# Moving the shifted copies of score bits from GpSimd to VectorE in a two-attention kernel

## The chip, the cores and the metric

The kernel runs on one core of a Trainium2 chip. The time is the device time of one execution in microseconds (us). Before the change three runs gave 713.89, 715.19 and 715.36 us; their median is 715.19 us. The profile is of one further execution, whose span is 713.4 us.

## The reference

Two attention layers with 2048 positions, model width 448 and 16 heads of 28 are computed and laid side by side in the output.

```python
# A: 16 query heads share one key head and one value head
q = heads(x @ wq); k = x @ wk; v = x @ wv
p = softmax(q @ k.T * 28 ** -0.5)           # over all 2048 keys
a = (p @ v).reshape(1, 2048, 448) @ wo
# B: each position looks at itself and 7 earlier ones, 2 apart
q, k, v = heads(x @ wqkv)
logits = where(idx >= 0, q . k[idx] * 28 ** -0.5, -1e9)   # idx = pos - 2 * (0..7)
b = (softmax(logits) @ v[idx]).reshape(1, 2048, 448) @ wo
out = concatenate([a, b], axis=-1)
```

Inputs and output are bf16.

## The kernel before

Attention A is done in 16 *groups*: four chunks of 512 queries by four sets of four heads. A group has 64 *jobs*, one per head and block of 128 keys. A job is one score matmul (line 1119) that fills one PSUM bank with 128 keys by 512 queries; the four heads sit in four strips of 32 rows, so that up to four jobs run side by side in the array. A 29th row of the operands adds a term from the query's squared norm (line 652 squares it); the key side holds a one in that row.

A bank of scores goes one of two ways. ScalarE takes the exponential of three banks or of two banks in one activation (line 924) into the tile P. VectorE instead builds the exponential from bits: line 1155 adds a bias to the scores, clips at zero and stores int16 values, which read as bf16 are powers of two with a straight line between them. Three *shifted copies* of these bits, plus 32, plus 64 and plus 96, are made in tile Z: line 1163 makes the first from the base (512 elements in each partition), and line 1170 makes the other two from the first two (1024 elements). Each of the four versions goes through a value matmul with its own weighted set of values, and the four sums together approximate the exponential closely. So a job on ScalarE costs TensorE one value matmul (line 1218) and a job on VectorE four. Banks 0 to 2 and 3 to 4 are two rings for ScalarE; banks 5 to 7 are *flexible* and serve VectorE's score banks, the value sums and the projections. The tile P has 8 slots and Z has 6. About every fourth or fifth bank goes to VectorE (DRATE, line 34, and `want_d`, line 1132).

Attention B has 16 such groups as well, with banded masks added by a matmul (line 1078) and small score matmuls (line 1092). Its key eviction (line 688) multiplies by a column that blanks the unused rows and adds a column that puts the one into each head's 29th row; the columns are operands in SBUF. Query evictions (line 658) multiply by such a column too.

At the end of a group the value sums are copied out (line 728), the denominators go by small transfers through a reciprocal (line 747) and back as a broadcast, a product normalizes them (line 778), four output projections follow, and their results are cast (line 818) and stored.

No loop of the chip sets the order. A planner in Python keeps a clock for each engine and lets the engine with the earliest clock choose its next piece of work (`loop`, line 856). Work is listed with the engines that may do it, a priority and a planned duration in nanoseconds. Each engine then runs its list strictly in the planned order, and waits on semaphores where an operand comes from another engine. Planned durations that are off therefore do not make a result wrong, but leave an order that does not fit. For the first copy the plan says 560 on GpSimd and 215 on VectorE, and for the second 1.7 times that; squares have 620 and normalizations 1150 on GpSimd (GP_S1, GP_TT16, GP_TT32, lines 42 to 44). GpSimd or VectorE may take these, VectorE only when GpSimd's clock is far ahead (`hold`, in `spec_choose`, line 876). TensorE chooses in `pe_choose` (line 1270): a score batch whose banks are free goes first, and the rest fills the time until ScalarE would run dry.

Of the kernel before, what the change touches and what calls it, by code (L numbers as in the profile page):

```python
# [15 lines left out]
DH = 28  # L16
# [21 lines left out]
TOL = 40.0  # L38
FTOL = 250.0
EXPC = 0.8333  # L40
EXP0 = 52.0
GP_S1 = 560.0
GP_TT16 = 620.0
GP_TT32 = 1150.0
# [40 lines left out]
class Spec:  # L85


    def __init__(self, engs, reads, writes, make, prio, dur, gate, name, hold):
        self.engs = engs
        self.reads = reads  # L90
        self.writes = writes
        self.make = make
        self.prio = prio
        self.dur = dur
        self.gate = gate
        self.name = name
        self.hold = hold

# [32 lines left out]
class _Gen:  # L131
    def __init__(self, nc, A_x, A_wq, A_wk, A_wv, A_wo, B_x, B_wqkv, B_wo, out):
        self.nc = nc
        self.A_x, self.A_wq, self.A_wk, self.A_wv, self.A_wo = A_x, A_wq, A_wk, A_wv, A_wo
        self.B_x, self.B_wqkv, self.B_wo = B_x, B_wqkv, B_wo
        self.out = out
        self.ops = []
        self.T = {e: 0.0 for e in ("pe", "act", "dve", "gp", "sp")}
        self.mode = None
        self.pend = []  # L140
        self.fills = []
        self.cur = None
        self.actq = []
# [16 lines left out]
    def put(self, eng, emit, dur, took, reads=(), writes=(), appends=(), dma=False, name=""):  # L160
        o = Op()
        o.eng, o.emit, o.dma, o.name = eng, emit, dma, name
        deps = {}
        for res in reads:
            for d in res.w:
                deps[d] = True
        for res in writes:
            for d in res.w:
                deps[d] = True
            for d in res.r:  # L170
                deps.setdefault(d, False)
        for res in appends:
            for d in res.r:
                deps.setdefault(d, False)
        t = self.T[eng]
        for d, full in deps.items():
            if d.eng != eng or d.dma:
                t = max(t, d.done + SEM)
            elif full and eng != "pe":
                t = max(t, d.done + SELF)  # L180
        o.deps = [d for d, full in deps.items() if d.eng != eng or d.dma or (full and eng != "pe")]
        o.start = t
        o.done = t + took
        self.T[eng] = t + dur
        o.busy = dur

        def note(lst):
            if not dma:
                for i, x in enumerate(lst):
                    if x.eng == eng and not x.dma:  # L190
                        lst[i] = o
                        return
            lst.append(o)

        for res in reads:
            note(res.r)
        for res in writes:
            res.w = [o]
            res.r = []
        for res in appends:  # L200
            note(res.w)
        o.idx = len(self.ops)
        self.ops.append(o)
        return o
# [109 lines left out]
    def alloc(self, es):  # L314
# [47 lines left out]
        self.zero = sb([128, 512], BF16, "zero")  # L362

# [5 lines left out]
    def plan_start(self):  # L369
        g = self  # L370
        put = self.put
        self.nswitch = 0
        R = {}
# [69 lines left out]
        for c in range(1, 4):  # L443
            for kt in range(4):
                c0 = 128 * kt if kt < 3 else D - 128
                self.dma_op("sp", g.xT_A[:, kt, 512 * c:512 * c + 512], g.A_x[0, 512 * c:512 * c + 512, c0:c0 + 128],
                            writes=[res("xA", c, kt)], transpose=True, issue=760, lands=2800, name="xAt")
        for c in range(4):
            par, half = c // 2, c % 2
            for kt in range(4):  # L450
                c0 = 128 * kt if kt < 3 else D - 128
                src = g.B_x[0, 1024 * half + par:1024 * half + 1024 - 1 + par:2, c0:c0 + 128]
                self.dma_op("sp", g.xT_B[:, kt, 512 * c:512 * c + 512], src,
                            writes=[res("xB", c, kt)], transpose=True, issue=760, lands=2800, name="xBt")

        def later():
# [7 lines left out]
            w3("gp", g.wB, g.B_wqkv, 0, 3 * D, "wB", [])  # L464
            gp(lambda e: e.memset(g.mask[:, :], 0.0), 450, writes=[res("m")])
# [28 lines left out]
    def evict(self, bank, make, engs=("dve",), dur=(600,), reads=(), writes=(), prio=2, last=True, cb=None, name=""):  # L494

        rd, wr = [bank.res] + list(reads), list(writes)

        def mk(eng, ns):
            if last:
                bank.busy = False  # L500
            return dict(emit=make, reads=rd, writes=wr, took=ns + 95, cb=cb)
        self.pend.append(Spec(engs, rd, wr, mk, prio, dict(zip(engs, dur)), None, name, False))

    def later(self, engs, dur, reads, make, prio=3, gate=None, name="", hold=False, writes=()):
        self.pend.append(Spec(engs, list(reads), list(writes), make, prio, dict(zip(engs, dur)), gate, name, hold))
# [10 lines left out]
    def make_fills(self):  # L516
# [30 lines left out]
        for c in range(4):  # L547
# [5 lines left out]
            def after(bank, c=c):  # L553
                self.evict(bank, lambda e: e.tensor_scalar(out=g.kT_A[:, 512 * c:512 * c + 512], in0=g.bank(bank.i), scalar1=g.col[:, 0:1],
                                                           scalar2=None, op0=ALU.add), ("dve",), (600,), reads=[res("c0")], writes=[res("kA", c)],
                           prio=0.5 if c == 0 else 1, name="ke")
# [71 lines left out]
        def q_fill(kind, key, s, gg, w, off, x, xk, c, due, enabled, elig=0.0):  # L628
# [10 lines left out]
            def after(bank):  # L639
                def cb(o):  # L640
# [13 lines left out]
                    if first and gg == 0:  # L654
                        self.later(("dve",), (345,), [res(r1, s, gg)], mk, prio=0.4, name="sq")
                    else:
                        self.later(("gp", "dve"), (GP_TT16, 345), [res(r1, s, gg)], mk, prio=2.5, name="sq", hold=True)
                self.evict(bank, lambda e: e.tensor_scalar(out=t[:, s, gg, :], in0=g.bank(bank.i), scalar1=g.col[:, 2:3], scalar2=None, op0=ALU.mult),  # L658
                           ("dve",), (600,), reads=[res("c2")], writes=[res(r1, s, gg), res(r2, s, gg)], prio=0.5 if first and gg == 0 else 2,
# [15 lines left out]
        for c in range(4):  # L675
# [3 lines left out]
            for gg in range(4):  # L679
# [7 lines left out]
                def after(bank, gg=gg, c=c):  # L687
                    self.evict(bank, lambda e: e.tensor_scalar(out=g.kT_B[:, gg, 512 * c:512 * c + 512], in0=g.bank(bank.i), scalar1=g.col[:, 1:2],  # L688
                                                               scalar2=g.col[:, 0:1], op0=ALU.mult, op1=ALU.add), ("dve",), (600,),
                               reads=[res("c0"), res("c1")], writes=[res("kB", c, gg)], prio=2, name="kBe",  # L690
                               cb=lambda o: self.kready.add((c, gg)))
                fill(f"kB{c}.{gg}", t0 - 13 + 4 * gg, steps, after, elig=t0 - 50)
            q_norms("B", c % 2, ("B", c), t0 - 6)
            for b in range(5):
# [11 lines left out]
                def after(bank, nk=nk, vs=vs, c=c, b=b):  # L706
                    self.evict(bank, lambda e: e.tensor_copy(out=g.vB[0:nk, vs, :, 0:DH],  # L707
                                                             in_=g.bank(bank.i, 0, nk, 0, D).rearrange("p (h d) -> p h d", d=DH)),
                               ("dve",), (540,), reads=[res("vB1")], writes=[res("vB", vs)], prio=2, name="vBe",
# [9 lines left out]
    def chain(self, key, bank, due):  # L719
# [44 lines left out]
        def mul(p, b):  # L764
            ok = (kind, c)

            def mk(eng, ns):
# [4 lines left out]
                def cb(o):  # L772
# [3 lines left out]
                    if self.odone[ok] == 4:  # L776
# [4 lines left out]
                       hold=True)  # L781
# [94 lines left out]
    def spec_choose(self, eng):  # L876
        T = self.T[eng]
        best = None
        for s in self.pend:
# [4 lines left out]
            if eng == "dve" and s.hold and T > self.T["gp"] - GP_AHEAD:  # L884
                continue
            if self.ready(eng, s.reads, s.writes) <= T + 15.0:
                best = s
# [6 lines left out]
    def do_spec(self, s, eng):  # L894
# [9 lines left out]
        else:  # L904
            op = self.put(eng, a["emit"], ns, a["took"], a["reads"], a["writes"], name=s.name)
# [111 lines left out]
    def qk_next(self):  # L1017
        ring = self.rings[self.ringi % 2]
        bj = self.b_next() if len(ring) == 2 else None
        if bj is not None:  # L1020
            jobs, kind = bj, "B"
            s = bj[0] % 2
            reads = [self.res("qB", s, bj[1]), self.res("qrB", s, bj[1]), self.res("kB", bj[0], bj[1]), self.res("m"), self.res("m0"), self.res("id")]
            if bj[0] % 2:
                reads.append(self.res("kB", bj[0] - 1, bj[1]))
# [38 lines left out]
    def do_qk(self, jobs, kind, reads):  # L1064
# [37 lines left out]
        dj = None  # L1102
        if self.want_d(T):
            ok = self.flex_free(T + 10)
            if ok:
                dj = self.d_job({j for _, _, j in jobs}, jobs)
        alljobs = list(jobs)
# [29 lines left out]
    def dread(self, job, bank):  # L1137
# [11 lines left out]
        def mk(eng, ns):  # L1149
            bank.busy = False  # L1150

            def cb(o):
                unit(0, zr[0])
                self.later(("gp", "dve"), (GP_S1, 215), [zr[0]], sh1, prio=1.2, name="s1", hold=True, writes=[zr[1]])
# [4 lines left out]
        def sh1(eng, ns):  # L1159
            def cb(o):  # L1160
                unit(1, zr[1])
                self.later((eng,), (ns * 1.7,), [zr[0], zr[1]], sh2, prio=1.1, name="s2", writes=[zr[2]])
            return dict(emit=lambda e: e.tensor_scalar(out=g.Z[:, z, 1, :], in0=g.Z[:, z, 0, :], scalar1=32.0, scalar2=None, op0=ALU.add),  # L1163
                        reads=[zr[0]], writes=[zr[1]], took=ns + 60, cb=cb)

        def sh2(eng, ns):
# [3 lines left out]
            return dict(emit=lambda e: e.tensor_scalar(out=g.Z[:, z, 2:4, :], in0=g.Z[:, z, 0:2, :], scalar1=64.0, scalar2=None, op0=ALU.add),  # L1170
# [99 lines left out]
    def pe_choose(self):  # L1270
        T = self.T["pe"]
        q = self.qk_next()
        if q is not None and q[1] and q[0] <= T + 30.0:
            self.do_qk(q[2], q[3], q[4])
            return
        idle = self.T["act"] + sum(EXPC * 512 * len(b) + EXP0 for b, _, _ in self.actq)
# [6 lines left out]
        room = horizon - T - sw  # L1283
        if pv and (len(pv) == 4 or press) and (room >= 217.0 - TOL or hard):
# [57 lines left out]
```

## Time and profile before

| engine | busy us | share | instructions |
|---|---|---|---|
| TensorE matmuls | 503.2 | 71% | 5268 |
| VectorE | 290.6 | 41% | 496 |
| ScalarE | 433.5 | 61% | 369 |
| GpSimd | 642.5 | 90% | 369 |

| operation | on | count | mean ns |
|---|---|---|---|
| first copy, line 1163 | GpSimd | 134 | 1503 |
| first copy, line 1163 | VectorE | 42 | 623 |
| second and third copy, line 1170 | GpSimd | 134 | 2783 |
| second and third copy, line 1170 | VectorE | 42 | 675 |
| score bits, line 1155 | VectorE | 176 | 688 |
| exponential, line 924 | ScalarE | 365 | 1247 |

The second table comes from the profile's groups: each has a line, an engine, an operation, the tiles written and read, and the mean duration of one instruction. Matmuls on TensorE are pipelined, so that their busy time holds latencies that overlap. The mean granted clock of TensorE was 0.756 of its full speed. An idle engine is not by itself a loss; what counts is what the engines that others wait for are waiting for.

### The profile page before, as it was taken

What the parts mean: (1) busy time and instruction counts of PE and PEld (TensorE: products, weight loads), DVE (VectorE), ACT (ScalarE), POOL (GpSimd) and SP (SyncE); (2) the same over time, 40 slices, a digit from 0 to 9 for tenths busy, and PEclk for the clock granted to TensorE, in tenths of its full rate; (3) what the DMA queues carried; (4) which work ended last, traced back from release to release, by engine and by line L of the source; (5) the groups of instructions that cost most, each with busy time, mean ns of one, the idle gap of its engine ahead of it and who ended that gap; (6) DMA issues with size and microseconds to landing.
All of it is one profiled execution on the core that took longest, in us unless ns stands there. A gap on an engine that the chain in (4) does not pass through costs nothing.

```text
span 713.4 us, 12414 instructions
## 1 busy us (share of the span) xinstructions
PE 503.2 (71%) x5268; PEld 141.2 (20%) x5268; DVE 290.6 (41%) x496; ACT 433.5 (61%) x369; POOL 642.5 (90%) x369
## 2 busy tenths in 40 slices
PE   6967775876788677779757658684758856556672
PEld 3311221211222122123212212221112201111111
DVE  5634514442542335325344625224433415364431
ACT  2965766664876567559758739374657636455450
POOL 7799949999699999998799999998999999999960
PEclk9988978886987678569989969677576865555556
DMA  9920001010010101001010100011001010000001
GB/s 180 142 53 17 2 1 41 10 33 1 18 54 28 35 1 33 2 17 36 24 32 28 34 16 17 7 30 38 10 24 36 8 42 0 10 7 1 16 1 42
DMA packets 37335, 20.10 MB, mean 28 GB/s; under 512 B 27552, under 2 KB 32736, under 8 KB 37280
## 3 DMA queue, kind: packets, MB, share of 16 engines
q1 hardware_dynamic: 35616, 16.84, 9.9%
q0 software_dynamic: 704, 2.03, 1.5%
q8 instruction: 42, 0.69, 0.4%
q10 hardware_dynamic: 960, 0.43, 0.3%
q14 instruction: 13, 0.11, 0.1%
HBM read 11.31 MB, written 3.93 MB: 21 GB/s over the span
## 4 chain that ended last, share of the span: by engine, by line
POOL 80%; PE 11%; issue 4%; DVE 3%; DMA 1%; POOLq 0%; ACTq 0%; ACT 0%; SPq 0%
POOL Z L1170 48%; POOL Z L1163 26%; PE ps L512 4%; POOL oTn L778 3%; PE ps L1218 3%; POOL sq L652 3%; PE ps L1119 2%; DVE Z L1155 1%; DMA bc<-rec_scratch 1%; DMA wq<-in_A_wq_dram 1%; PE ps L1078 1%; DVE qT_A L658 0%; PE ps L1092 0%; DVE PVs L728 0%; DVE ob L818 0%
## 5 line engine op out<-in xcount | busy, mean ns | idle before, releaser
L924 ACT ACTIVATE P<-ps 128x1536 bf16<-128x1536 f32 x365 | 431.0, 1247 | 253.4 <-PE ps L1119 204.4
L1170 POOL TENSOR_SCALAR Z<-Z 128x1024 int16<-128x1024 int16 x134 | 372.9, 2783 | 9.3
L1218 PE MATMUL ps<-Z,vA 128*32 128x512 bf16 x704 | 193.9, 493 | 126.7 <-POOL Z L1163 80.4
L1163 POOL TENSOR_SCALAR Z<-Z 128x512 int16<-128x512 int16 x134 | 201.4, 1503 | 21.3 <-DVE Z L1155 21.3
L1218 PE MATMUL ps<-P,vA 128*32 128x512 bf16 x848 | 191.6, 471 | 30.7 <-POOL Z L1170 18.1
L1155 DVE TENSOR_SCALAR Z<-ps 128x512 int16<-128x512 f32 x176 | 121.0, 688 | 223.4 <-PE ps L1119 223.0
L1119 PE MATMUL ps<-qT_A,kT_A 29*128 29x512 bf16 x1024 | 157.1, 465 | 12.1 <-DVE Z L1155 3.9
L1218 PEld LDWEIGHTS ps<-Z,vA 128*32 128x32 bf16 x704 | 40.2, 101 | 190.3 <-POOL Z L1163 87.1
L1119 PEld LDWEIGHTS ps<-qT_A,kT_A 29*128 29x128 bf16 x1024 | 34.4, 94 | 165.3 <-issue 80.2
L1218 PEld LDWEIGHTS ps<-P,vA 128*32 128x32 bf16 x848 | 40.7, 98 | 86.1 <-issue 40.7
L512 PE MATMUL ps<-xT_B,wB 128*32 128x512 bf16 x512 | 51.2, 447 | 1.0 <-DVE kT_B L688 0.8
L778 POOL TENSOR_TENSOR oTn<-PVs,bc 128x512 bf16<-128x512 f32 x24 | 30.5, 1272 | 14.1 <-DMA bc<-rec_scratch 14.1
L728 DVE COPY PVs<-ps 128x512 f32<-128x512 f32 x32 | 21.8, 687 | 49.9 <-PE ps L1218 35.5
L512 PE MATMUL ps<-woA,oTn 128*32 128x448 bf16 x256 | 26.8, 473 | 17.6 <-POOL oTn L778 17.4
L818 DVE CAST ob<-ps 128x448 bf16<-128x448 f32 x32 | 19.9, 621 | 44.8 <-PE ps L512 44.8
L1170 DVE TENSOR_SCALAR Z<-Z 128x1024 int16<-128x1024 int16 x42 | 28.3, 675 | 0.9
L512 PE MATMUL ps<-wB,xT_B 128*32 128x448 bf16 (+3 forms) x320 | 27.6, 413 | 0.2 <-DVE PVs L728 0.2
L1163 DVE TENSOR_SCALAR Z<-Z 128x512 int16<-128x512 int16 x42 | 26.2, 623 | 1.1
L512 PE MATMUL ps<-woB,oTn 128*32 128x448 bf16 x256 | 21.9, 406 | 5.3 <-POOL oTn L778 4.6
L1078 PE MATMUL ps<-mask,ident 128*128 128x512 bf16 x64 | 25.0, 482 | 0.1
L512 PE MATMUL ps<-xT_A,wq 128*32 128x512 bf16 x256 | 23.3, 428 | 0.6 <-DMA wq<-in_A_wq_dram 0.4
L707 DVE CAST vB<-ps 109x448 bf16<-109x448 f32 (+2 forms) x20 | 12.4, 618 | 24.6 <-PE ps L512 24.6
(81 smaller groups left out, 241.9 us busy)
## 6 DMA issues: line engine op xcount, KB each, us to landing
bc<-rec_scratch SPq DMA_DIRECT2D x32, 256.0 KB
out_dram<-ob SPq DMA_DIRECT2D x32, 112.0 KB, 1.7
den<-PVs SPq DMA_DIRECT2D x128, 2.0 KB, 1.7
wB<-in_B_wqkv_dram POOLq DMA_DIRECT2D x1, 1008.0 KB, 7.2
rec_scratch<-rec SPq DMA_DIRECT2D x32, 8.0 KB, 1.6
xn<-in_A_x_dram SPq DMA_DIRECT2D x4, 112.0 KB, 2.2
woA<-in_A_wo_dram POOLq DMA_DIRECT2D x4, 98.0 KB, 4.0
woB<-in_B_wo_dram POOLq DMA_DIRECT2D x4, 98.0 KB, 5.5
```

What stands on the lines that cost most here:

```text
L512: ins = e.matmul(self.bank(bank, 32 * j, 32 * j + m, 0, n), lhs(j), rhs(j), start=start, stop=stop, tile_position=(0, 32 * j))
L652: return dict(emit=lambda e: e.tensor_tensor(out=g.sq[:, z, gg, :], in0=t[:, s, gg, :], in1=t[:, s, gg, :], op=ALU.mult), reads=[res(r1, s ...
L728: return dict(emit=lambda e: e.tensor_copy(out=g.PVs[:, p, :], in_=g.bank(bank.i)), reads=[bank.res], writes=[self.pvs.res[p]], took=ns + ...
L778: return dict(emit=lambda e: e.tensor_tensor(out=g.oTn[:, z, gg, :], in0=g.PVs[:, p, :], in1=g.bc[:, b, :], op=ALU.mult), reads=[self.pvs. ...
L818: return dict(emit=lambda e: e.tensor_copy(out=g.ob[:, o_, :], in_=g.bank(bank.i, 0, 128, 0, D)), reads=[bank.res], writes=[self.outs.res[ ...
L924: self.put("act", lambda e: e.activation(g.P[:, k, 0:512 * n], g.ps[:, lo:lo + 512 * n], ACT.Exp, scale=ASCALE), ns, ns + 110, [self.banks ...
L1078: ins = e.matmul(g.bank(b), g.ident[:, :], (g.mask if half else g.mask0)[:, :], start=True, stop=False)
L1119: ins = e.matmul(g.bank(b), g.kT_A[32 * j:32 * j + DH + 1, 128 * tb:128 * tb + 128], g.qT_A[32 * j:32 * j + DH + 1, gr.sc % 2, gr.g, :], s ...
L1155: return dict(emit=lambda e: e.tensor_scalar(out=g.Z[:, z, 0, :], in0=g.bank(bank.i), scalar1=ZBIAS, scalar2=0.0, op0=ALU.add, op1=ALU.max ...
L1163: return dict(emit=lambda e: e.tensor_scalar(out=g.Z[:, z, 1, :], in0=g.Z[:, z, 0, :], scalar1=32.0, scalar2=None, op0=ALU.add), reads=[zr ...
L1170: return dict(emit=lambda e: e.tensor_scalar(out=g.Z[:, z, 2:4, :], in0=g.Z[:, z, 0:2, :], scalar1=64.0, scalar2=None, op0=ALU.add), reads ...
L1218: ins = e.matmul(g.bank(b, 32 * j, 32 * j + 32), l, r, start=st, stop=sp, tile_position=(0, 32 * j))
```

## The change

The shifted copies are made by VectorE, except for those of every twelfth bank (GP_EACH), which GpSimd makes. The planner is told that the two engines exclude each other in the copies, the squares and the normalizations (`port`: such an operation starts only after the last one of either engine), and is given other durations for GpSimd. The copies are written as a multiplication by one and an addition in one instruction. Query evictions use an immediate factor in place of a column (except in the first chunk), and B's key eviction becomes a plain copy, after which a small transfer writes the ones into the 29th rows. In `pe_choose` a score batch whose banks are free may wait for a flexible bank, so that a job for VectorE can go along with it, as long as ScalarE's backlog lasts (DWAIT); and a projection that was begun is carried on first if there is time. In the changed program 175 pairs of copies are on VectorE and 16 on GpSimd, and ScalarE has 359 exponentials.

```diff
+DWAIT = 100.0
-GP_S1 = 560.0
-GP_TT16 = 620.0
-GP_TT32 = 1150.0
+GP_S1 = 900.0
+GP_EACH = 12
+GP_TT16 = 1010.0
+GP_TT32 = 1230.0
...
     def put(self, eng, emit, dur, took, reads=(), writes=(), appends=(), dma=False, name="", port=False):
+        if port:
+            t = max(t, self.port)
+            self.port = t + dur
...
-                        self.later(("gp", "dve"), (GP_TT16, 345), [res(r1, s, gg)], mk, prio=2.5, name="sq", hold=True)
-                self.evict(bank, lambda e: e.tensor_scalar(out=t[:, s, gg, :], in0=g.bank(bank.i), scalar1=g.col[:, 2:3], scalar2=None, op0=ALU.mult),
+                        self.later(("gp", "dve"), (GP_TT16, 345), [res(r1, s, gg)], mk, prio=2.5, name="sq", hold=True, port=True)
+                sc1 = g.col[:, 2:3] if first else CQ
+                self.evict(bank, lambda e: e.tensor_scalar(out=t[:, s, gg, :], in0=g.bank(bank.i), scalar1=sc1, scalar2=None, op0=ALU.mult),
...
-                    self.evict(bank, lambda e: e.tensor_scalar(out=g.kT_B[:, gg, 512 * c:512 * c + 512], in0=g.bank(bank.i), scalar1=g.col[:, 1:2],
-                                                               scalar2=g.col[:, 0:1], op0=ALU.mult, op1=ALU.add), ("dve",), (600,),
+                            return dict(dma=True, out=g.kT_B[DH:128:32, gg, 512 * c:512 * c + 512], in_=g.one[0:4, :], reads=[res("one"), res("kB", c, gg)],
+                                        writes=[res("k1B", c, gg)], cb=lambda o: self.kready.add((c, gg)))
+                    self.evict(bank, lambda e: e.tensor_copy(out=g.kT_B[:, gg, 512 * c:512 * c + 512], in_=g.bank(bank.i)), ("dve",), (600,),
...
+            if s.port and eng in ("dve", "gp") and self.port > T + 15.0:
+                continue
...
-                self.later(("gp", "dve"), (GP_S1, 215), [zr[0]], sh1, prio=1.2, name="s1", hold=True, writes=[zr[1]])
+                en = ("gp",) if self.nD % GP_EACH == 5 else ("dve",)
+                self.later(en, (GP_S1 if en[0] == "gp" else 200,), [zr[0]], sh1, prio=1.2, name="s1", writes=[zr[1]], port=True)
...
-                self.later((eng,), (ns * 1.7,), [zr[0], zr[1]], sh2, prio=1.1, name="s2", writes=[zr[2]])
-            return dict(emit=lambda e: e.tensor_scalar(out=g.Z[:, z, 1, :], in0=g.Z[:, z, 0, :], scalar1=32.0, scalar2=None, op0=ALU.add),
+                self.later((eng,), (332 if eng == "dve" else 1.9 * ns,), [zr[0], zr[1]], sh2, prio=1.1, name="s2", writes=[zr[2]], port=True)
+            return dict(emit=lambda e: e.tensor_scalar(out=g.Z[:, z, 1, :], in0=g.Z[:, z, 0, :], scalar1=1.0, scalar2=32.0, op0=ALU.mult, op1=ALU.add),
...
-            return dict(emit=lambda e: e.tensor_scalar(out=g.Z[:, z, 2:4, :], in0=g.Z[:, z, 0:2, :], scalar1=64.0, scalar2=None, op0=ALU.add),
+            return dict(emit=lambda e: e.tensor_scalar(out=g.Z[:, z, 2:4, :], in0=g.Z[:, z, 0:2, :], scalar1=1.0, scalar2=64.0, op0=ALU.mult, op1=ALU.add),
...
+        idle = self.T["act"] + sum(EXPC * 512 * len(b) + EXP0 for b, _, _ in self.actq)
         if q is not None and q[1] and q[0] <= T + 30.0:
-            self.do_qk(q[2], q[3], q[4])
-            return
-        idle = self.T["act"] + sum(EXPC * 512 * len(b) + EXP0 for b, _, _ in self.actq)
+            if (q[3] == "B" or T + 40.0 > idle - QKLAT - DWAIT or not self.want_d(T) or self.flex_free(T + 10)
+                    or self.d_job({j for _, _, j in q[2]}, q[2]) is None):
+                self.do_qk(q[2], q[3], q[4])
+                return
+            q = (idle - QKLAT - DWAIT,) + q[1:]
...
+        if self.cur is not None and f is not None and room >= self.cur.list[self.cur.i][2] - TOL and not hard:
+            self.do_fill(f)
+            return
```

## The prediction

> **What bounds the kernel now.** I read five views in this order. First the page's busy times, slices and chain.
>
> ```profile
> PE 503.2 (71%) x5268; PEld 141.2 (20%) x5268; DVE 290.6 (41%) x496; ACT 433.5 (61%) x369; POOL 642.5 (90%) x369
> ...
> POOL 7799949999699999998799999998999999999960
> PEclk9988978886987678569989969677576865555556
> ...
> POOL 80%; PE 11%; issue 4%; DVE 3%; DMA 1%; POOLq 0%; ACTq 0%; ACT 0%; SPq 0%
> POOL Z L1170 48%; POOL Z L1163 26%; PE ps L512 4%; POOL oTn L778 3%; PE ps L1218 3%; POOL sq L652 3%; PE ps L1119 2%; DVE Z L1155 1%; DMA bc<-rec_scratch 1%; DMA wq<-in_A_wq_dram 1%; PE ps L1078 1%; DVE qT_A L658 0%; PE ps L1092 0%; DVE PVs L728 0%; DVE ob L818 0%
> ```
>
> GpSimd works 90% of the span, full in nearly every slice, and 80% of the chain that ended last is GpSimd; three quarters of the span is two lines, 1170 and 1163, the shifted copies. Second, the cost groups for those lines on both engines:
>
> ```profile
> L924 ACT ACTIVATE P<-ps 128x1536 bf16<-128x1536 f32 x365 | 431.0, 1247 | 253.4 <-PE ps L1119 204.4
> L1170 POOL TENSOR_SCALAR Z<-Z 128x1024 int16<-128x1024 int16 x134 | 372.9, 2783 | 9.3
> ...
> L1163 POOL TENSOR_SCALAR Z<-Z 128x512 int16<-128x512 int16 x134 | 201.4, 1503 | 21.3 <-DVE Z L1155 21.3
> ```
>
> One pair of copies costs GpSimd 1.50 + 2.78 = 4.28 us, and 134 pairs cost 574 us. Its idle time ahead of them is 31 us, so it is simply full. Third, the waits:
>
> ```profile
> ACT P L924 <- PE ps L1119: 204.4, 109, 8.6
> PEld ps L1218 <- POOL Z L1163: 103.0, 37, 7.8
> ...
> PEld ps L1218 <- POOL Z L1170: 80.2, 50, 3.2
> ```
>
> TensorE's queue is in order: a value matmul (line 1218) that waits for a Z copy holds back the score matmuls (1119) behind it, so ScalarE starves for 204 us. GpSimd's backlog becomes idle time of TensorE and ScalarE. Fourth, what VectorE pays for the same two operations, per line the shortest, median and longest in ns:
>
> ```profile
> L1163 DVE TENSOR_SCALAR Z<-Z x42: 277/542/1179, 14.1 to 683.1; 128x512 int16<-128x512 int16 x42
> L1170 DVE TENSOR_SCALAR Z<-Z x42: 378/668/1369, 14.4 to 683.8; 128x1024 int16<-128x1024 int16 x42
> ```
>
> Even its slowest copy beats GpSimd's. In the trace many first copies took 0.29 us and many second ones 0.43 us; the longer ones met a GpSimd operation. Fifth, slices of 20 us (busy us and instruction counts in the order PE, weight loads, DVE, ACT, POOL, then clock): all seven whose granted clock is above 0.9, that is where TensorE was least starved.
>
> ```profile
> 20.00:40.00 20.00, 16.78 (x311) 5.91 (x303) 14.14 (x31) 18.88 (x17) 14.92 (x14) 0.97 0.93 135
> 100.00:120.00 20.00, 16.53 (x216) 5.27 (x204) 10.22 (x18) 16.74 (x15) 15.82 (x9) 0.92 0.07 16
> 200.00:220.00 20.00, 16.00 (x202) 4.88 (x199) 7.93 (x13) 15.21 (x14) 19.61 (x11) 0.93 0.14 44
> 260.00:280.00 20.00, 17.26 (x220) 5.44 (x220) 10.69 (x18) 17.88 (x17) 18.06 (x10) 0.99 0.07 19
> 320.00:340.00 20.00, 18.55 (x253) 6.18 (x251) 11.18 (x19) 18.96 (x18) 16.94 (x9) 0.96 0.13 39
> 340.00:360.00 20.00, 16.46 (x200) 5.10 (x200) 7.87 (x14) 15.84 (x15) 15.60 (x10) 0.91 0.06 16
> 380.00:400.00 20.00, 15.90 (x225) 5.13 (x224) 11.84 (x21) 16.76 (x16) 19.48 (x10) 1.00 0.12 35
> ```
>
> ScalarE does 17+15+14+17+18+15+16 = 112 exponentials there, 16.0 per 20 us, and up to 18; over the whole span it does 365 x 20 / 713 = 10.2. That is the gap to close.
>
> **What the Trainium skill says.** "VectorE: DVE Perf Modes", The perf-mode tier table: a tensor_scalar on 16-bit data in SBUF can run at 4 elements a cycle. The trace agrees in kind: 512 more elements add 0.13 to 0.15 us (0.28 or 0.29 against 0.41 to 0.43), a quarter of what one element a cycle at that page's 0.96 GHz would take. "SBUF — State Buffer", Who interferes with whom: VectorE in such a mode and GpSimd lock each other out, for the whole instruction. The trace agrees in part: first copies on VectorE that start early in a 2.77 us copy of GpSimd end about 1.18 us after its start, others of 0.29 us lie wholly inside one, so it holds the port for about its first 0.89 us only. "GPSIMD Engine Reference", Engine selection, calls one-input operations there roughly line-rate; 1.50 us for 512 elements does not agree. "TensorE: Matmul & The Clock Gate", Part 1: the clock halves when TensorE idles for some 3.4 us. The trace agrees: the clock row falls to 5 at the end, where GpSimd is full.
>
> **The change part by part.** The instruction order of the changed program, which can be read without a run, gives the counts.
>
> *Removed from GpSimd:* 134 copy pairs become 16: 16 x 4.28 = 69 us. Its tensor products grow from 20 squares and 24 normalizations to 29 and 32: 29 x 1.04 + 32 x 1.27 = 71 us. With some 20 us of set-up it has 160 us of work. It stops being a bound whatever the new two-operation form costs there (if it halves the price, another 35 us fewer).
>
> *Added to VectorE:* 42 pairs become 175. Unhindered, 175 x (0.29 + 0.43) = 126 us, against 54.5 us now (26.2 + 28.3): +72. Bound below: the shortest, 0.28 + 0.38, 116 us. Bound above: the means of now, 0.62 + 0.68, as if GpSimd were as full as now, 228 us. I take 126, since GpSimd's load falls by three quarters and the new order also keeps the two apart. Multiply-then-add instead of an add: line 1155 (add, then max, 0.688 us) costs the same as the plain copy of line 728 (0.687 us), so the second operation is free. Banks evaluated by VectorE rise from 176 to 191: +15 x 0.69 = +10. Nine squares and eight normalizations leave it: -4 - 7. Evictions: 28 lose the column operand (0.73 to 0.69) and 16 lose two (0.81 to 0.69): -1 - 2. Sum 290.6 + 72 + 10 - 11 - 3 = 359 us.
>
> *ScalarE:* 359 exponentials instead of 365 (179 wide, 180 narrow): 433.5 - 6 x 1.18 = 426 us busy. In the timeline 16 in a row took 18.34 us, 1.15 each: floor 359 x 1.15 = 411 us.
>
> *TensorE:* 60 more value matmuls, four at a time and about 0.22 us a round at full clock in the timeline: +3 us. Its load at full clock is about 503.2 x 0.756 + 3 = 383 us (an estimate, since busy time holds latencies too). Not a bound, if the clock follows.
>
> *The wait for a bank:* a score batch may now hold TensorE's queue until ScalarE's backlog is nearly used up. Behind it are value matmuls and ScalarE. Cost between 0 and 0.1 us (the 100 of the planner's constant) for each of some 327 batches, 33 us. I take 4 us, since it acts only where a bank is missing; it buys the 15 banks that ScalarE no longer does. The trace of before has nothing like it.
>
> *The 16 row copies of ones:* one small transfer behind each key eviction, about 0.6 us of the queue (the broadcast's issue takes 0.58) and 1.7 us to land (the den transfers). The scores of the second attention now wait for it; hidden, because its queries' norm rows already take the same route and the keys are made groups ahead. I take 0.
>
> *The sum:* the first exponential starts at 12.9 us, and the last ends 21.9 us before the end (691.5 of 713.4: the last group's normalization, transfers and output). Both stay: 34.8 us. Between them, 359 exponentials at 16.0 per 20 us take 448.8 us. 448.8 + 34.8 + 4 = 488 us. At ScalarE's floor it would be 411 + 34.8 = 446 us.
>
> **The rivals.**
> *ScalarE's rate sets it, as above:* 488 us, between 455 (18 per 20 us gives 399, below the floor, so floor plus 9) and 520 (359 at 14.8 per 20 us, near the poorer of the slices). For it: GpSimd was still 75 to 98% busy in those slices, and ScalarE ran at that rate even so. Against it: they are the best third.
> *VectorE becomes the bound:* copies at their present means give 359 + 102 = 461 us of work. At 90% use, 512 + 35 = 547 us. For it: a bank needs three dependent operations in order on VectorE, and evictions queue behind them. Against it: GpSimd's load falls.
> *TensorE stays at its low clock:* 503 + 3 us busy at 18.55 of 20, the most any slice shows, is 546 + 35 = 581 us. Against it: the clock is high exactly where work is dense.
> *Slower than before:* all copies at VectorE's longest, 175 x (1.18 + 1.37) = 446, with 359 - 126 = 233 us of other work: 679 us of VectorE, and 679 / 0.97 + 35 = 735 us. Against it: those maxima come only from meeting GpSimd operations, which become rare; also possible if the new form missed the fast mode and met them.
>
> **How the numbers follow.** ScalarE's rate 0.66, VectorE 0.22, TensorE's clock 0.08, slower 0.03, and 0.01 for no change. The predicted time is 488. The range 455 to 540 holds the first case and most of the VectorE case, whose milder forms lie below 547. Faster is 0.96, same 0.01, slower 0.03.
>
> **What would show it.** Right: GpSimd below 180 us busy and gone from the chain; VectorE's copies at medians near 0.29 and 0.43 us; exponentials starved for 30 to 80 us instead of 253; the clock above 0.9; a chain that mixes ScalarE, TensorE and VectorE. Wrong: copies on VectorE above 0.6 us; waits of value matmuls for VectorE's Z lines of over 100 us in all; score matmuls waiting long for ScalarE with ScalarE idle, which would be the bank wait. The forecast fails if several nearly full engines in a fixed order wait for each other more than the seven slices show.

## The result and the profile after

The changed kernel takes 471.73 us, median of four runs (470.95 to 477.38), against 715.28 us for the kernel before, the median of four runs too. The ratio is 0.660, with a 95% interval of 0.6545 to 0.6664. The forecast was 488 us in a range of 455 to 540. Times here and below are medians of all executions, while the ratios leave out some that ran over 1.5% above the fastest of their kernel, so that the two can differ in the third digit.

The page of the changed kernel, in the same rows as those shown of before:

```profile
PE 408.7 (87%) x5313; PEld 130.6 (28%) x5313; DVE 344.5 (73%) x760; ACT 412.9 (88%) x363; POOL 122.6 (26%) x151
...
POOL 8751320432503025251111523311132011120201
PEclk9799999999999999999999999999989789999956
...
PE 31%; ACT 27%; DVE 19%; DMA 11%; issue 6%; SPq 2%; POOL 2%; POOLq 0%; ACTq 0%; DVEq 0%
...
L940 ACT ACTIVATE P<-ps 128x1536 bf16<-128x1536 f32 x359 | 410.3, 1276 | 29.5 <-PE ps L1141 27.4
...
L1193 DVE TENSOR_SCALAR Z<-Z 128x1024 int16<-128x1024 int16 x175 | 79.3, 463 | 1.4
...
L1186 DVE TENSOR_SCALAR Z<-Z 128x512 int16<-128x512 int16 x175 | 57.9, 348 | 0.9
```

GpSimd fell from 642 to 123 us and from 80% of the chain to 2%. The exponentials (now line 940) were idle ahead of their starts for 29.5 us in all instead of 253. The clock row reads 9 nearly everywhere until the end. ScalarE is now the fullest engine by busy time (88%), with TensorE at 87% and VectorE at 73% behind it. The chain is a mixture of these three, with TensorE at 31% and ScalarE at 27%.

One stretch of the timeline shows the new steady state, 22 exponentials on end with no idle time between them, 1.14 us each:

```profile
39.54 25.05 ACT L940 ACTIVATE P<-ps 128x1024 bf16<-128x1024 f32 x22
```

The first surprise is in the two copy lines of the new profile, per engine as shortest, median and longest in ns:

```profile
L1186 DVE TENSOR_SCALAR Z<-Z x175: 226/284/2075, 18.7 to 442.4; 128x512 int16<-128x512 int16 x175
L1186 POOL TENSOR_SCALAR Z<-Z x16: 609/617/726, 30.0 to 433.4; 128x512 int16<-128x512 int16 x16
...
L1193 DVE TENSOR_SCALAR Z<-Z x175: 362/417/2470, 19.1 to 442.7; 128x1024 int16<-128x1024 int16 x175
L1193 POOL TENSOR_SCALAR Z<-Z x16: 1044/1044/1143, 30.7 to 434.2; 128x1024 int16<-128x1024 int16 x16
```

VectorE's copies are what the forecast took, 0.28 and 0.42 us. GpSimd's are not: a pair that cost it 4.28 us now costs 1.66. The data and shapes are the same; only the operation is written differently, as multiply by one and add instead of add. So two edits of the change can each have emptied GpSimd: the move to VectorE, and the form. The experiments take them apart.

### The profile page after: what moved, and what is told of

Same layout as the page of the kernel before. It is cut to its first block, busy times and chain, and to the rows that moved or that the text cites. A ratio compares the mean times of both kernels' runs of the same rounds, so it can differ in the third digit from the quotient of the medians.

```text
span 469.2 us, 12573 instructions
## 1 busy us (share of the span) xinstructions
PE 408.7 (87%) x5313; PEld 130.6 (28%) x5313; DVE 344.5 (73%) x760; ACT 412.9 (88%) x363; POOL 122.6 (26%) x151
## 4 chain that ended last, share of the span: by engine, by line
PE 31%; ACT 27%; DVE 19%; DMA 11%; issue 6%; SPq 2%; POOL 2%; POOLq 0%; ACTq 0%; DVEq 0%
ACT P L940 27%; PE ps L522 10%; PE ps L1141 9%; PE ps L1241 9%; DVE Z L1178 8%; DMA bc<-rec_scratch 5%; DVE Z L1193 4%; DVE Z L1186 4%; DMA rec_scratch<-rec 3%; PE ps L1094 2%; SPq L221 2%; PE ps L1108 1%; DMA den<-PVs 1%; POOL oTn L792 1%; DMA wq<-in_A_wq_dram 1%
## 5 line engine op out<-in xcount | busy, mean ns | idle before, releaser
L940 ACT ACTIVATE P<-ps 128x1536 bf16<-128x1536 f32 x359 | 410.3, 1276 | 29.5 <-PE ps L1141 27.4
L1241 PE MATMUL ps<-Z,vA 128*32 128x512 bf16 x764 | 149.5, 396 | 4.0 <-POOL Z L1186 2.2
L1241 PE MATMUL ps<-P,vA 128*32 128x512 bf16 x833 | 146.4, 393 | 4.6 <-ACT P L940 1.7
L1141 PE MATMUL ps<-qT_A,kT_A 29*128 29x512 bf16 x1024 | 130.9, 393 | 17.8 <-ACT P L940 9.3
L1193 DVE TENSOR_SCALAR Z<-Z 128x1024 int16<-128x1024 int16 x175 | 79.3, 463 | 1.4
L1186 DVE TENSOR_SCALAR Z<-Z 128x512 int16<-128x512 int16 x175 | 57.9, 348 | 0.9
L1186 POOL TENSOR_SCALAR Z<-Z 128x512 int16<-128x512 int16 x16 | 10.2, 636 | 91.6 <-DVE Z L1178 91.6
L662 POOL TENSOR_TENSOR sq<-qT_A 128x512 bf16<-128x512 bf16 x13 | 14.0, 1081 | 49.8 <-DVE qT_A L669 49.8
L522 PE MATMUL ps<-wB,xT_B 128*32 128x448 bf16 (+2 forms) x320 | 21.8, 356 | 1.3 <-DVE vB L721 1.0
L662 POOL TENSOR_TENSOR sq<-qT_B 128x512 bf16<-128x512 bf16 x16 | 17.0, 1064 | 12.7 <-DVE qT_B L669 12.7
```

The lines of the kernel that those rows point to most:

```text
L522: ins = e.matmul(self.bank(bank, 32 * j, 32 * j + m, 0, n), lhs(j), rhs(j), start=start, stop=stop, tile_position=(0, 32 * j))
L662: return dict(emit=lambda e: e.tensor_tensor(out=g.sq[:, z, gg, :], in0=t[:, s, gg, :], in1=t[:, s, gg, :], op=ALU.mult), reads=[res(r1, s ...
L940: self.put("act", lambda e: e.activation(g.P[:, k, 0:512 * n], g.ps[:, lo:lo + 512 * n], ACT.Exp, scale=ASCALE), ns, ns + 110, [self.banks ...
L1141: ins = e.matmul(g.bank(b), g.kT_A[32 * j:32 * j + DH + 1, 128 * tb:128 * tb + 128], g.qT_A[32 * j:32 * j + DH + 1, gr.sc % 2, gr.g, :], s ...
L1241: ins = e.matmul(g.bank(b, 32 * j, 32 * j + 32), l, r, start=st, stop=sp, tile_position=(0, 32 * j))
```

## The experiments

Ratios are to the kernel before, run on the same chip in the same session (718 to 719 us there), with 95% intervals.

**The form alone** (kernel before, order untouched):

```diff
-scalar1=32.0, scalar2=None, op0=ALU.add)
+scalar1=1.0, scalar2=32.0, op0=ALU.mult, op1=ALU.add)
-scalar1=64.0, scalar2=None, op0=ALU.add)
+scalar1=1.0, scalar2=64.0, op0=ALU.mult, op1=ALU.add)
```

> The kernel before with one edit: both shifted copies are written as multiply by one, then add, as in the changed kernel. Order and counts of all engines stay those of before (134 pairs on GpSimd, 42 on VectorE). Theory 'engine' (the prediction's: a pair costs GpSimd 4.28 us in either form, and the gain comes from moving it): about 715 us, GpSimd 642 us busy. Theory 'form' (GpSimd is slow only at the one-operation form; a pair costs it 0.62 + 1.04 = 1.66 us, as in the profile after): GpSimd 642 - 134 x 2.62 = 291 us busy and no bound, 475 to 520 us.

Measured: 509.6 us, ratio 0.707 (0.7027 to 0.7112). The copies of that run, all still on the engines where they were:

```profile
L1163 POOL TENSOR_SCALAR Z<-Z x134: 612/621/1052, 32.7 to 487.8; 128x512 int16<-128x512 int16 x134
L1163 DVE TENSOR_SCALAR Z<-Z x42: 278/580/1128, 13.3 to 488.4; 128x512 int16<-128x512 int16 x42
...
L1170 POOL TENSOR_SCALAR Z<-Z x134: 1042/1047/1315, 33.4 to 488.6; 128x1024 int16<-128x1024 int16 x134
L1170 DVE TENSOR_SCALAR Z<-Z x42: 384/427/1414, 13.7 to 488.7; 128x1024 int16<-128x1024 int16 x42
```

Two edited lines, with no instruction moved, bring 208 of some 245 us. GpSimd was busy for 298.9 us, and the exponentials were idle ahead of their starts for 65.3 us instead of 253.4. My theory, that a pair costs GpSimd 4.28 us in either form, falls.

**All but the form** (changed kernel with the old form; the diff is the one above, reversed). This run keeps the move, the new planned durations, the exclusion, the bank wait and the new evictions; the move was not run without the rest.

> The changed kernel with the copies written as one addition, as before; order unchanged. Both theories put GpSimd's 16 pairs at 4.28 us each, 42 us more, in an engine that idles for 347 us. Theory 'engine': 472 us within 5, since VectorE's own copies cost the same in both forms (0.28 and 0.42 us). Theory 'form' with a large part of the gain in VectorE's form: VectorE's copies get slower than 0.3 and 0.45 us and the time rises over 490 us.

Measured: 487.3 us, ratio 0.678 (0.6730 to 0.6824), some 13 us slower than the changed kernel, where I had expected at most 5. VectorE's copies in that run, and GpSimd's:

```profile
L1186 DVE TENSOR_SCALAR Z<-Z x175: 228/284/1351, 17.2 to 455.6; 128x512 int16<-128x512 int16 x175
L1186 POOL TENSOR_SCALAR Z<-Z x16: 1484/1490/1742, 28.6 to 445.8; 128x512 int16<-128x512 int16 x16
...
L1193 DVE TENSOR_SCALAR Z<-Z x175: 361/419/1514, 17.5 to 455.9; 128x1024 int16<-128x1024 int16 x175
L1193 POOL TENSOR_SCALAR Z<-Z x16: 2769/2770/2946, 30.4 to 447.4; 128x1024 int16<-128x1024 int16 x16
```

VectorE's medians don't depend on the form (284 and 419 against 284 and 417). What remains are 16 long pairs on GpSimd in an order planned for shorter ones. The idle time ahead of the exponentials is 40.4 us instead of 29.5, and GpSimd is busy 165.4 us instead of 122.6. The weight loads of value matmuls wait 12.0 us for GpSimd's copies instead of 3.4, and 41 of VectorE's copies took over 30 ns more than their median instead of 29; how the 13 us split between these the run doesn't show. So even 16 operations on an engine that idles two thirds of the time cost something. The bound goes without the form too: 134 pairs on GpSimd became 16. The form alone, or everything but the form, removes it.

**The plan's durations alone** (kernel before, old form):

```diff
-GP_S1 = 560.0
-GP_TT16 = 620.0
-GP_TT32 = 1150.0
+GP_S1 = 1490.0
+GP_TT16 = 1040.0
+GP_TT32 = 1270.0
...
-self.later((eng,), (ns * 1.7,), [zr[0], zr[1]], sh2, ...
+self.later((eng,), (1.86 * ns if eng == "gp" else 365,), [zr[0], zr[1]], sh2, ...
```

> The kernel before, one-operation copies, with only the planner's durations for GpSimd corrected to what the profile before shows (copy 1490 and 1.86 times that, squares 1040, products 1270). The planner then puts 71 pairs on GpSimd and 91 on VectorE, and 370 exponentials on ScalarE. Theory 'a wrong plan was the loss': GpSimd 71 x 4.28 + 37 = about 340 us busy, 480 to 530 us. Theory 'engine' in its strict form (the two engines must be kept apart, and all copies be moved): over 580 us.

Measured: 524.6 us, ratio 0.731 (0.7273 to 0.7340), as the theory of the wrong plan has it. The planner of before believed 560 for a copy that took 1490, and so kept sending work to a full engine. With the real price it splits the pairs 71 to 91, and GpSimd is busy for 347.5 us:

```profile
L1163 DVE TENSOR_SCALAR Z<-Z x91: 223/315/1244, 15.7 to 498.8; 128x512 int16<-128x512 int16 x91
L1163 POOL TENSOR_SCALAR Z<-Z x71: 1479/1490/1767, 33.6 to 498.3; 128x512 int16<-128x512 int16 x71
```

So this edit works by moving copies as well: 63 pairs leave GpSimd, 49 more are on VectorE, and 14 banks go to ScalarE. Moving about half of the old, dear copies away is enough to bring 194 us. The old plan's 560 and 952 ns lie close to what the new form takes (617 and 1044): that plan fitted the form that it didn't use.

**Is it the second operation, or multiply and add?** (kernel before)

```diff
-scalar1=32.0, scalar2=None, op0=ALU.add)
+scalar1=32.0, scalar2=0.0, op0=ALU.add, op1=ALU.add)
...
+scalar1=64.0, scalar2=0.0, op0=ALU.add, op1=ALU.add)
```

> The kernel before with the copies written as add 32 (or 64), then add zero. If GpSimd's price hangs on there being a second operation, a pair costs it 1.6 to 1.7 us and the time is that of the run with multiply and add. If it hangs on the multiply-add pair itself, a pair stays near 4.28 us and the time near 715 us.

Measured, one execution: 883.2 us, and GpSimd busy for 815.3 us.

```profile
L1163 POOL TENSOR_SCALAR Z<-Z x134: 1917/1922/2409, 32.9 to 853.2; 128x512 int16<-128x512 int16 x134
L1163 DVE TENSOR_SCALAR Z<-Z x42: 275/294/1426, 13.7 to 850.0; 128x512 int16<-128x512 int16 x42
...
L1170 POOL TENSOR_SCALAR Z<-Z x134: 3621/3629/4077, 34.9 to 855.2; 128x1024 int16<-128x1024 int16 x134
```

Both branches of the expectation missed: a second addition makes it dearer than one, while multiply and add is the cheap form. So of these three forms it is the pair of operations that counts and not their number. VectorE is again indifferent (medians 294 and 427). The run also shows the mechanism from its other side: with GpSimd dearer, ScalarE starves for score matmuls for 341.9 us, where it was 204.4 before.

**Copies back on GpSimd, all else kept** (changed kernel, new form, real price in the plan):

```diff
-en = ("gp",) if self.nD % GP_EACH == 5 else ("dve",)
+en = ("dve",) if self.nD % GP_EACH == 5 else ("gp",)
-GP_S1 = 900.0
+GP_S1 = 620.0
...
-1.9 * ns
+1.69 * ns
```

> The changed kernel with the copies of eleven banks of twelve on GpSimd (176 pairs, at its real price in the plan) and of every twelfth on VectorE (16): the move undone, all else kept, the two-operation form too. GpSimd gets 176 x 1.66 + 73 + 20 = 385 us of work. Theory 'the form and the plan made the gain, not the move': 465 to 490 us. Theory 'the move made a good part': value matmuls wait for GpSimd's Z lines for over 100 us, and the time is over 500 us.

Measured: 478.3 us, ratio 0.663 (0.6587 to 0.6669); GpSimd is busy for 377.5 us and VectorE for 252.4:

```profile
PE 421.4 (88%) x5316; PEld 133.9 (28%) x5316; DVE 252.4 (53%) x443; ACT 413.9 (86%) x363; POOL 377.5 (79%) x471
```

The weight loads of value matmuls wait 14.5 us for GpSimd's copies, and not over 100. The changed kernel's intervals (0.6545 to 0.6664, and 0.6563 to 0.6615 in a second session) overlap this one. With the form and the rest of the change in place, where the copies run is worth about half a per cent by these ratios, and 1.6% at the far ends of the intervals. The move that names the change is not needed for the gain.

The form alone left 509.6 us, and this run 478.3. The 31 us between them come from the plan's durations, the exclusion, the bank wait, the evictions and the projection that is carried on first, together. The next runs leave some of these out one by one. The plan's durations were not put back in the changed kernel, and the projection rule was never run by itself.

**The rest of the change.** The base is the changed kernel once more:

> The changed kernel once more, as the base of the three runs beside it: 470 to 474 us on every theory.

Measured: 473.4 us, ratio 0.659 (0.6563 to 0.6615).

*Without the bank wait:*

```diff
-            if (q[3] == "B" or T + 40.0 > idle - QKLAT - DWAIT or not self.want_d(T) or ...):
-                self.do_qk(q[2], q[3], q[4])
-                return
-            q = (idle - QKLAT - DWAIT,) + q[1:]
+            self.do_qk(q[2], q[3], q[4])
+            return
```

> The changed kernel without the wait of score batches for a flexible bank. The planner then gives VectorE 174 banks and ScalarE 914 instead of 897. Theory 'ScalarE sets the end': 17 more banks at 0.44 us are 7.5 us more of ScalarE, 477 to 483 us. Theory 'the wait costs ScalarE idle time' (the prediction's 4 us, up to 33): removing it gives that back, 465 to 474 us.

Measured: 484.5 us, ratio 0.673 (0.6701 to 0.6764), 11 us slower. ScalarE's busy time rises from 413.3 to 420.7 us with the 17 banks it gets, which is the larger part of that. So the wait earns about 10 us, give or take a few, since the executions spread from 477.0 to 488.2 us; and it costs none that shows: ScalarE's idle time between its first and last exponential is about 23 us in both traces.

*Without the exclusion in the plan:*

```diff
-        if port:
+        if False:
...
-if s.port and eng in ("dve", "gp") and self.port > T + 15.0:
+if False and eng in ("dve", "gp") and self.port > T + 15.0:
```

> The changed kernel with a planner that doesn't keep the two engines apart (the flag is ignored); 180 pairs on VectorE, 17 on GpSimd. GpSimd is busy 26% of the span, so at random about one VectorE copy in four meets one of its operations, at 0.3 to 1 us each: some 50 to 90 meetings, 20 to 60 us more of VectorE busy time. Theory 'the exclusion matters': ScalarE starves and the time is 485 us or more. Theory 'it hardly matters, since GpSimd has little left': 468 to 480 us.

Measured: 490.3 us, ratio 0.681 (0.6784 to 0.6835), 17 us slower. Its waits and busy times:

```profile
ACT P L940 <- PE ps L1141: 41.8, 38, 5.9
...
PE 422.1 (86%) x5331; PEld 131.9 (27%) x5331; DVE 367.4 (75%) x781; ACT 413.3 (84%) x361; POOL 118.9 (24%) x148
```

VectorE is busy 28 us longer than in the base (367.4 against 339.2), with about 7 us of it for six more banks. In its trace 53 copies of VectorE took over 30 ns more than their median, in the base's 28. ScalarE starved 41.8 us for score matmuls instead of 27.0. So keeping the engines apart in the plan is worth 17 us here, more than the bank wait.

*Evictions by columns, without the row copies of ones:*

```diff
-                sc1 = g.col[:, 2:3] if first else CQ
+                sc1 = g.col[:, 2:3]
...
-lambda e: e.tensor_copy(out=g.kT_B[...], in_=g.bank(bank.i))        # and the transfer of ones
+lambda e: e.tensor_scalar(out=g.kT_B[...], in0=g.bank(bank.i), scalar1=g.col[:, 1:2], scalar2=g.col[:, 0:1], op0=ALU.mult, op1=ALU.add)
```

> The changed kernel with the evictions of queries and of the second attention's keys by columns, as before, and so without the 16 row copies of ones. VectorE works 3 us more. Theory 'ScalarE sets the end': hidden, 470 to 475 us. If the row copies delayed the second attention's scores: 1 to 4 us faster.

> The run with the evictions by columns once more, as a base: ratio to before 0.648 to 0.653 if its gain over the changed kernel (0.659) is real; 0.656 to 0.662 if it was chance.

> The changed kernel with the key eviction by columns and no row copies of ones; query evictions keep the immediate. Theory 'the row copies cost time' (they stand in order in the transfer queue ahead of the normalization's transfers): as fast as the run with all columns, ratio 0.648 to 0.654. Theory 'something else in that run': 0.656 to 0.662, as the changed kernel.

Measured: with all columns 469.0 us, ratio 0.6505 (0.6478 to 0.6533) beside the base, and in another session 469.7 us, ratio 0.6544 (0.6510 to 0.6577). With columns for the keys only: 470.6 us, ratio 0.6539 (0.6507 to 0.6571). All three are below the changed kernel's 0.659 and 0.660; the first is clear of the base's interval, the other two overlap it. So undoing this part is likely worth 3 to 6 us, and undoing it for the keys alone brings as much. The waits of the transfer queue in the base name a candidate:

```profile
SPq L221 <- DVE PVs L742: 74.8, 16, 14.1
...
SPq L221 <- DVE kT_B L704: 27.7, 8, 7.1
```

The queue stood 27.7 us behind key evictions, in order ahead of the transfers that normalize a group. The traces speak against it: with all columns that wait is gone, but the queue waits as long in all (281.9 us against 280.7), and GpSimd waits as long for the broadcasts (179.0 us against 179.7). Nor does any matmul of the second attention show a wait for the ones. The edit also changes the planned order a little, so the cause stays open. The version by columns is the fastest that was measured, if only by this margin.

*GpSimd at its real price, every sixth bank* (on top of key columns):

```diff
-GP_S1 = 900.0
-GP_EACH = 12
+GP_S1 = 620.0
+GP_EACH = 6
...
-1.9 * ns
+1.69 * ns
```

> Evictions of keys by columns, and GpSimd at its real price in the plan (620 and 1.69 times that) and for every sixth bank in place of every twelfth: 35 pairs there, 164 on VectorE, 889 banks on ScalarE in place of 897. Theory 'ScalarE sets the end': 8 banks at 0.44 us are 3.6 us fewer, ratio 0.643 to 0.649. Theory 'more meetings of the two engines cost more than that': 0.652 or more.

Measured: 480.3 us, ratio 0.668 (0.6643 to 0.6723): slower, against my expectation from ScalarE's work alone. ScalarE starved 34.9 us for score matmuls, against 25.2 with all columns and 30.9 with columns for the keys in the same session. 43 of VectorE's copies took over 30 ns more than their median, against 29 and 28. I can't say which of the two, the meetings or the other order, cost more; it stays open.

## Why the forecast held, and what in it was off

*GpSimd is the bound, and starves ScalarE through TensorE's queue.* Right. Three runs that shorten GpSimd's work by different edits (the form alone, all but the form, the plan's durations alone) bring 208, 231 and 194 us, and ScalarE's starving for score matmuls falls from 204 us to 52, 35 and 64. The one that makes the copies dearer raises it to 342.

*ScalarE sets the end afterwards.* Right in kind: it is the fullest engine, though it shares the chain with TensorE and VectorE. The first exponential starts at 13.6 us, the last ends at 447.4, and 21.8 us follow: 35.4 us at the two ends where I took 34.8. Between them 359 exponentials took 433.8 us, 16.55 per 20 us where I took 16.0. This is the term that was mis-sized, by 15 us. Likely the seven slices of before from which I took the rate were themselves still held up by GpSimd, which was 75 to 98% busy there. ScalarE's busy time is 412.9 us and not 426; I had priced an exponential by the mean of before, 1.18 us, and they now take 1.14 where they follow one another. The floor that I derived, 446 us, was not reached.

*The bank wait costs 4 us.* Wrong sign. It earns about 10 us, most of which I had counted in the 359 exponentials.

*GpSimd's price in the new form.* Wrong, though it didn't show in the sum. I read that VectorE's second operation is free and let GpSimd keep 4.28 us a pair "whatever the new two-operation form costs there". It has 16 pairs at 1.66, and 122.6 us of work instead of 160. What I got wrong with it is the reason for the gain: I took the move for necessary. That the time came out inside the range doesn't speak for the move, since the form alone, at 509.6 us, lies inside it too.

*VectorE's work, 359 us.* Measured 344.5. The copies came out at 137 us instead of 126, since some still meet GpSimd (means 0.348 and 0.463, medians 0.284 and 0.417), which lies inside my bounds. The rest came out lower because VectorE's operations overlap in the records: their durations add up to 387.2 us for 344.5 us of busy time (before, 305.5 and 290.6). The sum of durations overstates a fuller engine.

*TensorE, about 383 us at full clock.* Measured 408.7 at a clock of 0.955, that is 390. The clock followed, as I had assumed: over whole runs the mean granted clock is higher where more matmuls are done per us, 0.696 at 6.0 (two additions), 0.756 at 7.4 (before), 0.884 at 10.2 (the form alone) and 0.955 at 11.3.

*GpSimd holds VectorE for its first 0.89 us only.* The "only" is wrong. A 2.77 us copy on GpSimd holds VectorE's copies a second time before it ends, as the last section shows. The sum of 126 us didn't rest on it, since it took VectorE's copies as unhindered.

*Row copies at nothing.* Probably 3 to 6 us too low, as told above.

The rivals: VectorE as the bound didn't come, as its copies kept their short medians. The low clock didn't either. What was missing was the rival that mattered: that the form of the operation alone could do it. The prediction allowed for a cheaper form on GpSimd, but only for the 16 pairs left there, and did not ask what it would do for all 134.

## What to carry to other kernels

When an engine is full of one operation, ask first what that operation costs there in another form, before asking where else it could run: the form took two lines and gave five sixths of the gain. An order planned ahead is as good as its durations; compare each planned number with the profile's median, since an operation that the plan prices too low overloads its engine. And when a change holds several edits that act on the same bound, test each alone and each left out, because they don't add up: here the form alone gave 208 us, all but the form 231, and everything together 245.

## What the runs showed of the hardware

GpSimd's price for a copy of int16 values hangs on the pair of operations, in the three forms that were run. From 512 to 1024 elements in each partition multiply-then-add adds 427 ns (617 to 1044), one addition 1281 ns (1487 to 2768), and two additions 1707 ns (1922 to 3629): 0.83, 2.50 and 3.33 ns an element, 1 to 3 to 4. The Trainium skill, "GPSIMD Engine Reference", Engine selection, calls one-input work there roughly line-rate; of the three forms at most the first fits that. VectorE shows no such difference: typically 0.28 to 0.29 and 0.42 to 0.43 us unhindered in each form. Why the forms differ on GpSimd no run shows.

How long such a copy holds VectorE's copies can be read off by when they start. These are from the run with the plan's durations alone, around one second-and-third copy of GpSimd, with no other operation of GpSimd behind it for 4.5 us:

```profile
384.51 2.77 POOL L1170 TENSOR_SCALAR Z<-Z 128x1024 int16<-128x1024 int16 x1
384.70 0.99 DVE L1163 TENSOR_SCALAR Z<-Z 128x512 int16<-128x512 int16 x1
385.73 0.43 DVE L1170 TENSOR_SCALAR Z<-Z 128x1024 int16<-128x1024 int16 x1
386.79 0.63 DVE L1163 TENSOR_SCALAR Z<-Z 128x512 int16<-128x512 int16 x1
```

The first of VectorE's copies, begun 0.19 us in, ends 1.18 us in; the next runs at its unhindered 0.43 us; the last, begun 2.28 us in, ends at 2.91. In this run's trace, beside second-and-third copies of GpSimd that took their usual 2.77 us, first copies on VectorE begun up to 0.87 us in end near 1.18, those begun from 0.89 to 1.26 us in take their 0.28 to 0.29 us, those begun from 1.84 to 2.46 us in end near 2.91, and those begun from 2.64 us in on run unhindered. With 0.29 us taken off the ends, GpSimd holds VectorE up to about 0.89 us, and again up to about 2.62 from 1.84 at the latest. With two additions (3.63 us) the stretches end at 0.89 and 3.48 us, and copies begun between 1.05 and 2.23 us in run unhindered. In the form multiply-then-add (1.05 us) there is one stretch, to about 0.90 us. So the dear forms keep GpSimd busy longer and hold VectorE twice.
